# A first chunk of 128 whole tokens and 256 split ones for 384 whole ones, the sign of the weights by ScalarE, packed left-over values, queries by tile, and new due dates

## The chip, the cores and the metric

One core of one Trainium2 chip. The metric is the device time of one execution in microseconds (us). Three runs of the kernel before gave 630.63, 631.63 and 631.82 us: a median of 631.63.

TensorE (PE) multiplies, VectorE (DVE), ScalarE (ACT) and GpSimd (POOL) do the elementwise work, and SyncE (SP) issues the DMAs. Each engine takes its own instructions in the order of the program.

## What is computed

Attention over pooled keys and values, then a channel mix with a token shift. There are 8 batches of 576 tokens, 8 heads of 64; 8 keys (and values) are averaged into one, which leaves 72.

```
k_p = k.reshape(B, H, Sp, pool, D).mean(axis=3)
v_p = v.reshape(B, H, Sp, pool, D).mean(axis=3)
attn = softmax(scale * q @ k_p.T)
x = (attn @ v_p)                      # as (B, S, 512)
x_prev = x shifted by one token, zero at the start of a batch
xk = mu_k * x + (1.0 - mu_k) * x_prev
xr = mu_r * x + (1.0 - mu_r) * x_prev
k = np.maximum(xk @ w_k, 0.0)         # 512 -> 1024
v = k * k @ w_v                       # 1024 -> 512
r = 1.0 / (1.0 + np.exp(-(xr @ w_r)))
return r * v
```

The weights come as float64 words.

## The kernel before

The 4608 tokens are one row, cut into 12 chunks of 384 (`CHUNKS`, L32); a chunk is 3 tiles of 128. For each tile, `softmax` (L600) multiplies queries and keys into the bank `sc` (L620), takes maxima (L633), subtracts (L651), exponentiates (L656) and normalizes (L670, L676); `transposed` (L684) and `transposed_rest` (L714) turn the probabilities of the first 64 keys (`pm`) and of the 8 left-over keys (`px`) over. For each chunk, `attended` (L762) multiplies them with the values (L794), `shifted` (L801) scales by 1 - mu (ScalarE, L807), shifts, and joins with mu times x (VectorE, L826). `hidden` (L848) is the product with w_k (L870), with relu (L880) and square (L884 or L887); `gate` (L901) that with w_r (L919) and the sigmoid; `mixed` (L931) that with w_v (L951), then the product with the gate (L960) and the store (L964).

A matmul is done in one of two ways. **Split**: each operand is kept as a high part, rounded to the type fp32r, and the rest as a low part, and three matmuls (high x high, low x high, high x low) are summed. **Whole**: one fp32 matmul, which the trace shows as two records. Split operands need work elsewhere: `x_parts` (L838) rounds on ScalarE (L842) and subtracts on GpSimd (L844); the hidden values are rounded (L893) and subtracted (L895); each of the 20 weight tiles goes through `split` (L478; L491 and L494). Chunk 0 is whole (`WHOLE`, L35), so that it can start before the weights are split; the others are split.

Each weight tile lands as float64 words and goes through `convert` (L447) first: ScalarE takes the absolute value of the upper word, scaled (L460); VectorE shifts it (L462), joins the sign of the upper word to it (L464), and joins the bits of the lower word (L469). Whole matmuls read the result (`got_wk`, `got_wr`, `got_wv`).

The means over 8 are sums: by TensorE with a unit matrix (`summed`, L503 to L512), or by three halvings on VectorE or GpSimd (L501), as `SUM_BY` says. The left-over values (`vr`) come as three copies in 96 partitions. Loads go through SP in the order of `LOADS` (L39), keys and values into one of three `stage` buffers or into `early` ones, which use tiles of later chunks.

The order on each engine is no code order. `Order` (L112 to L213) runs all steps as threads: among the steps that could start next on an engine, that with the lowest due date goes first, and a fixed program for each engine comes out. A step's due date is worked out from its chunk, plus its entry in `EARLIER`. Of all TensorE steps those of later chunks' softmax and attended values are dated `SPARE` after their inputs.

## Time and profile before

| | us |
|---|---|
| median of the runs shown | 631.63 (630.63 to 631.82) |
| span of the profiled execution, first to last instruction | 629.5 |
| PE busy / weight loads | 615.7 / 533.1 |
| DVE / ACT / POOL busy | 402.1 / 354.6 / 208.2 |
| chain that ended last, by line | L951 32%, L870 29%, L919 14%, L794 5%, L620 5% |

The profiled execution's own time is not listed apart; against the three runs, 1.1 to 2.3 us lie around its span. Matmuls are pipelined and their ends are modelled, so a busy TensorE row says that matmuls follow each other and not how fast; the distance between starts says that. A row "x64 | 21.9, 491 | 2.3" is a count, busy us, mean ns of one, and the idle us ahead of them with what ended it.

### The profile page before, as it was taken

How to read it: one execution, taken by the hardware profiler on the slowest of the kernel's cores; microseconds unless marked ns; L12 is line 12 of the kernel's file. 1: busy time of each engine (PE TensorE's matmuls, PEld its weight loads, DVE VectorE, ACT ScalarE, POOL GpSimd, SP SyncE). 2: the span in 40 equal slices, each digit the busy share in tenths (PEclk: the TensorE clock that was granted, in tenths of full speed). 3: DMA queues.
4: the chain of work that ended last, by engine and by line, in shares of the span. 5: the costliest groups of instructions: out<-in, count | busy, mean ns of one | idle time of the engine just before them, and what ended most of it. 6: DMA issues, size and time to landing. Idle time of an engine off the chain costs nothing.

```text
span 629.5 us, 8993 instructions
## 1 busy us (share of the span) xinstructions
PE 615.7 (98%) x3210; PEld 533.1 (85%) x3210; DVE 402.1 (64%) x786; ACT 354.6 (56%) x778; POOL 208.2 (33%) x324
## 2 busy tenths in 40 slices
...
GB/s 315 340 403 171 34 35 51 35 76 142 94 51 158 59 51 51 2 143 108 18 18 51 42 187 55 3 18 56 133 98 33 35 18 33 18 2 33 18 2 50
DMA packets 34989, 50.92 MB, mean 81 GB/s; under 512 B 6528, under 2 KB 22912, under 8 KB 34944
## 3 DMA queue, kind: packets, MB, share of 16 engines
...
q14 instruction: 20, 0.16, 0.1%
...
## 4 chain that ended last, share of the span: by engine, by line
PE 88%; DMA 6%; DVE 5%; SPq 1%; issue 0%; DVEq 0%
PE mm L951 32%; PE mm L870 29%; PE mm L919 14%; PE bank L794 5%; PE sc L620 5%; DMA got_wk<-in_w_k 4%; PE bank L695 2%; DMA got_wv<-in_w_v 1%; DVE tmp L464 1%; DVE got_wr L469 1%; PE bank L750 1%; SPq L421 0%; DVE got_wv L469 0%; DVE tmp L462 0%; DVE ptl L708 0%
## 5 line engine op out<-in xcount | busy, mean ns | idle before, releaser
L870 PE MATMUL mm<-xkh,w_k 128*128 128x384 f32 x704 | 182.3, 339 | 0.0
L951 PE MATMUL mm<-w_v,sh 128*128 128x512 f32 x528 | 171.7, 393 | 0.0
L870 PEld LDWEIGHTS mm<-xkh,w_k 128*128 128x128 f32 x704 | 125.6, 188 | 1.5 <-issue 0.6
L870 PE MATMUL mm<-xkl,w_k 128*128 128x384 f32 x352 | 118.0, 335 | 0.0
L951 PEld LDWEIGHTS mm<-w_v,sh 128*128 128x128 f32 x528 | 99.3, 188 | 19.5
L951 PE MATMUL mm<-w_v,sl 128*128 128x512 f32 x264 | 103.1, 390 | 0.0
L919 PE MATMUL mm<-w_r,xrh 128*128 128x512 f32 x264 | 86.3, 397 | 0.0
L807 ACT ACTIVATE t<-bank,om_sb 128x384 f32<-128x384 f32 x96 | 49.1, 580 | 46.7 <-PE bank L794 46.6
L893 ACT CAST sh<-rk 128x384 fp32r<-128x384 f32 x88 | 45.2, 513 | 51.9 <-DVE rk L887 51.4
L670 POOL TENSOR_TENSOR px<-e,sm 128x64 f32<-128x64 f32 x31 | 9.6, 310 | 189.8 <-DVE sm L664 189.8
L960 DVE TENSOR_TENSOR rs<-mm,rs 128x512 f32<-128x512 f32 x36 | 24.7, 687 | 74.7 <-PE mm L951 74.6
L826 DVE SCALAR_TENSOR_TENSOR xm<-bank,mu_sb,t 128x384 f32<-128x384 f32 x88 | 51.1, 612 | 31.8 <-POOL t L819 15.4
L895 DVE TENSOR_TENSOR sl<-rk,sh 128x384 fp32r<-128x384 f32 x88 | 53.3, 610 | 21.3 <-ACT sh L893 21.2
L870 PEld LDWEIGHTS mm<-xkl,w_k 128*128 128x128 f32 x352 | 66.1, 188 | 0.0
L887 DVE SCALAR_TENSOR_TENSOR rk<-mm,rk 128x384 f32<-128x384 f32 x88 | 48.5, 552 | 22.7 <-ACT rk L880 21.9
L501 POOL TENSOR_TENSOR stage<-stage 128x512 f32<-128x512 f32 (+5 forms) x60 | 52.9, 887 | 25.5 <-DMA stage<-in_vm 14.8
L844 POOL TENSOR_TENSOR xkl<-xm,xkh 128x384 fp32r<-128x384 f32 x44 | 45.5, 1034 | 48.0 <-ACT xkh L842 47.6
L919 PEld LDWEIGHTS mm<-w_r,xrh 128*128 128x128 f32 x264 | 49.7, 188 | 10.1
L951 PEld LDWEIGHTS mm<-w_v,sl 128*128 128x128 f32 x264 | 49.7, 188 | 8.9
L880 ACT ACTIVATE rk<-mm 128x384 f32<-128x384 f32 x88 | 42.9, 487 | 22.1 <-PE mm L870 21.1
L919 PE MATMUL mm<-w_r,xrl 128*128 128x512 f32 x132 | 51.5, 390 | 0.0
L620 PE MATMUL sc<-kbd,qs 128*128 128x144 f32 (+1 forms) x312 | 40.6, 289 | 5.4 <-ACT e L642 3.2
...
## 6 DMA issues: line engine op xcount, KB each, us to landing
out<-rs SPq DMA_DIRECT2D x36, 256.0 KB, 2.0
stage<-in_kT SPq DMA_DIRECT2D x15, 576.0 KB, 4.9
qs<-in_qT SPq DMA_DIRECT2D x32, 256.0 KB, 3.3
stage<-in_vm SPq DMA_DIRECT2D x14, 512.0 KB, 5.4
got_wk<-in_w_k SPq DMA_DIRECT2D x8, 512.0 KB, 10.0
got_wv<-in_w_v SPq DMA_DIRECT2D x8, 512.0 KB, 10.1
...
got_wr<-in_w_r SPq DMA_DIRECT2D x4, 512.0 KB, 9.7
```

Source lines behind the costliest of these rows:

```text
L501: nc_eng.tensor_tensor(out=st[:, :, :w], in0=st[:, :, :w], in1=st[:, :, w:2 * w], op=ALU.add)
L620: nc.tensor.matmul(out=halves[g // 2][o:o + n, 0, k:k + 2 * KEYS], lhsT=qs[:, g, o:o + n], rhs=kbd[b % 2][:, g, :], start=True, stop=True,)
L807: nc.scalar.activation(out=t[:, m, 1:n + 1], in_=xp, func=AF.Copy, scale=om_sb[:, m, g:g + 1])
L826: nc.vector.scalar_tensor_tensor(out=xm[:, :n], in0=xp, scalar=mu_sb[:, m, g:g + 1], in1=t[:, m, :n], op0=ALU.mult, op1=ALU.add,)
L844: nc.gpsimd.tensor_tensor(out=lo, in0=xm[:, :n], in1=hi, op=ALU.subtract)
L870: nc.tensor.matmul(out=hp, lhsT=w[:, o], rhs=x[:, ct, :n], start=(ct == 0 and k == 0), stop=(ct == NCT - 1 and k == len(terms) - 1),)
L880: nc.scalar.activation(out=rk[:, :n], in_=hp, func=AF.Relu)
L887: nc.vector.scalar_tensor_tensor(out=rk[:, :n], in0=hp, scalar=0.0, in1=rk[:, :n], op0=ALU.max, op1=ALU.mult)
L893: nc.scalar.copy(out=sh[:, :n], in_=rk[:, :n])
L895: nc.vector.tensor_tensor(out=operand("sl", c)[:, jt, :n], in0=rk[:, :n], in1=sh[:, :n], op=ALU.subtract)
L919: nc.tensor.matmul(out=bank, lhsT=x[:, ct, o], rhs=w, start=(ct == 0 and k == 0), stop=(ct == NCT - 1 and k == len(terms) - 1),)
L951: nc.tensor.matmul(out=bank, lhsT=s[:, o], rhs=w, start=(jt == 0 and k == 0), stop=(jt == NJT - 1 and k == len(terms) - 1),)
```

## The change

Chunk 0 is cut in two: 128 tokens, whole, and 256, split. `WHOLE_ATT` keeps attended values whole for both; the other products of the 256 are split. The whole chunk's operands now lie in two of the three stage buffers, which hold no load until its gate and its mix are done. The sign of a weight comes from ScalarE: Prelu with a slope of -2^32 for Abs, which shows up in the bits that the shift leaves, and VectorE's instruction at L464 goes. The left-over values of the first two batches come packed in 128 partitions (128 KB each) and are summed by two matmuls. Queries come by tile in one DMA. Tile 0's softmax is done in two halves. Keys summed on VectorE or GpSimd go straight to their place (L674). The joins of the whole chunk are dated apart (`later_joined`). Constants come in one DMA, some costs of the planner differ, and all due dates are new.

```diff
-CHUNKS = [384] * 12
+CHUNKS = [128, 256] + [384] * 11
...
 WHOLE = (0,)
+WHOLE_ATT = (0, 1)
+TWICE = 3
+PACKED = (0, 1)
+SPREAD_ON_ACT = (0,)
+HALVED = (0,)
+EARLY = (("sl", 2), ("xrl", 1))
...
+    "k0 k1 r1 c0 r0 q0 wk0 q1 v0 q2 v1 wk1 wk2 wk3 wk4 q4 k2 q3 wk5 k3 wk6 wk7 wr0 wr1 wr2 wr3 q5 "
+    "wv2 wv0 wv1 wv3 wv4 wv5 wv6 v3 v2 wv7 "
...
-SUM_BY = {
-    "k0": "t", "k1": "v", "v0": "t", "v1": "t", "r0": "t", "k2": "v", "k3": "v", "v2": "g", "v3": "v",
-    "r1": "g",
+SUM_BY = {"k0": "t", "k1": "v", "v0": "t", "v1": "t", "r0": "t", "k2": "g", "k3": "v", "v2": "g", "v3": "v", "r1": "g"}
...
-BY_HEAD = (0, 2)
-SQUARED_ON_ACT = 8
+BY_HEAD = ((0, 1),)
+SQUARED_ON_ACT = (8, 0)
...
-    "transposed_rest 6": 4.1, "hidden 2 5": -6.4, "convert r 1": -3.5, "mixed 0 1": -9.9,
+    "warm": 898.1, "constants": 928.6, "complements": 703.7, "loads": 690.8, "keys 0 0": 871.9,
...
-SPARE = 2.4
-SECOND = 13.3
-FIRST = 22.0
+PLAN = ""
+SPARE = 0.5
+SECOND = 0.0
+NEXT = 14.0
+ATT = [0.0, 10.0]
+FIRST = 15.0
...
+    packed = {0: const.tile([P, 2, 2, D], F32, name="packed")}
-    vbd_w = sb.tile([P, NPAIR, P], F32, name="vbd_w", tag="xkl")
+    vbd_w = sb.tile([P, NPAIR, P], F32, name="vbd_w", tag="ptl")
...
-    slots("stage", 3, [P, 2 * POOL * KEYS])
+    stage = [const.tile([P, 2 * POOL * KEYS], F32, name=f"stage{i}") for i in range(3)]
+    order.give("stage", stage[0])
+    first = CHUNKS[0]
+    whole_x = stage[1][:, :2 * NPAIR * (first + 1)].rearrange("p (m g n) -> p m g n", m=2, g=NPAIR)
+    whole_operands = {
+        "xkh": whole_x[:, 0], "xrh": whole_x[:, 1],
+        "sh": stage[2][:, :NJT * first].rearrange("p (j n) -> p j n", j=NJT),
+        "pth": const.tile([P, NPAIR, first], F32, name="whole_pth"),
+        "ptr": const.tile([REM, 2, first], F32R, name="whole_ptr"),
...
+            nc.sync.dma_start(out=given, in_=consts)
...
-            yield "sp", 0.6 * len(tiles[i][2]), False
-            for b, s, n, o in tiles[i][2]:
-                nc.sync.dma_start(out=qs[:, :, o:o + n], in_=qT[b, :, :, s:s + n])
+            yield "sp", 0.6, False
+            nc.sync.dma_start(out=qs, in_=qT[i])
...
+        if kind == "r" and i in PACKED:
+            st = None
+            if i not in packed:
+                st = yield take("stage")
+                packed[i] = st[:, :4 * D].rearrange("p (k g n) -> p k g n", k=2, g=2)
+            yield "sp", 0.6, False
+            nc.sync.dma_start(out=packed[i], in_=vp[PACKED.index(i)])
+            held["r", i] = st
+            order.fetched(("r", i), 128)
...
-        nc.scalar.activation(out=ff, in_=top.bitcast(F32), func=AF.Abs, scale=REBASE)
+        nc.scalar.activation(out=ff, in_=top.bitcast(F32), func=AF.Prelu, scale=REBASE, alpha=-2.0 ** 32)
         yield "dve", 0.335, True
         nc.vector.tensor_scalar(out=t, in0=t, scalar1=3, scalar2=None, op0=ALU.logical_shift_left)
-        yield dve(WP)
-        nc.vector.scalar_tensor_tensor(
-            out=t, in0=top, scalar=-0x80000000, in1=t, op0=ALU.bitwise_and, op1=ALU.bitwise_or
-        )
...
+        eng = SUM_BY.get(f"k{2 * b + p}", "v")
+        if eng != "t":
+            raw, v = held.pop(("k", 2 * b + p))
+            on = nc.vector if eng == "v" else nc.gpsimd
+            for n in (4, 2):
+                yield (dve if eng == "v" else pool)(2 * n * KEYS)
+                halve(on, v, KEYS, n)
+            yield ("dve", 0.284, True) if eng == "v" else ("pool", 0.87, True)
+            for h2 in range(2):
+                r = slice(h2 * D, (h2 + 1) * D)
+                on.tensor_tensor(
+                    out=kbd[b % 2][r, gs, h2 * KEYS:(h2 + 1) * KEYS],
+                    in0=v[r, :, :KEYS], in1=v[r, :, KEYS:2 * KEYS], op=ALU.add,
+                )
+            done_with("stage", raw)
+            order.make(("keys", b, p))
+            return
...
+    def value_parts(b, p):
+        i, gs = b % 2, slice(2 * p, 2 * p + 2)
+        yield need(("values", b, p), ("values clear", 1))
+        yield act(2 * P)
+        nc.scalar.copy(out=vbd_h[i][:, gs], in_=vbd_w[:, gs])
+        yield dve(2 * P)
+        nc.vector.tensor_tensor(
+            out=vbd_l[i][:, gs], in0=vbd_w[:, gs], in1=vbd_h[i][:, gs], op=ALU.subtract
+        )
+        order.make(("value parts", b, p))
...
+        if b in PACKED:
+            kind, raw = "mm", (yield take("mm"))
+            yield pe(2 * D, True, 2)
+            o = raw[:REM, :2 * D].rearrange("p (g n) -> p g n", g=2)
+            for k in range(2):
+                nc.tensor.matmul(out=o, lhsT=pick, rhs=packed[b][:, k], start=(k == 0), stop=(k == 1))
...
+        if b in SPREAD_ON_ACT:
+            yield "act", 0.84, False
+            for o in range(4):
+                nc.scalar.activation(
+                    out=vbd_r[i][:, :, o], in_=vq, func=AF.Copy, scale=mask_sb[:, o:o + 1]
+                )
...
+            yield from part(i, 0, 1)
+        else:
+            yield from part(i, 0, 2)
...
+    def part(i, a0, a1):
+        parts, na = tiles[i][2], a1 - a0
+        mine = slice(a0, a1)
+        yield need(("scoring", i))
+        sc, pair, halves = held["halves", i]
+        yield need(*[("keys", b, p) for b, *_ in parts for p in range(a0, a1)])
...
-        twice = c <= 1
+        on_act = i in COPIES_ON_ACT
+
+        twice = i < TWICE
...
+        bank = yield take("mm" if c in WHOLE and g == NPAIR - 1 else "bank")
+        t = None if c in WHOLE else (yield take("t"))
...
+        ts = [operand(f"x{'kr'[m]}h", c)[:, g] if whole else t[:, m] for m in range(2)]
...
+    def later_joined(c, g):
+        yield need(("x", c, g, 0))
+        yield from joined(c, g, 1)
...
+    def joined(c, g, m):
+        n = CHUNKS[c]
+        whole = c in WHOLE
+        bank, t = held["t", c, g]
+        if whole:
+            xm = operand(f"x{'kr'[m]}h", c)[:, g]
+            ts = xm[:, :n]
+        else:
+            xm = yield take("xm")
+            ts = t[:, m, :n]
+        yield "dve", 0.134 + n / 960, False
+        nc.vector.scalar_tensor_tensor(
+            out=xm[:, :n], in0=bank[:, :n], scalar=mu_sb[:, m, g:g + 1], in1=ts, op0=ALU.mult, op1=ALU.add,
+        )
...
-        yield need(("full" if whole else "parts", "k", jt))
+        yield need(("full" if whole else "parts", "k", jt), *([("x", c, 0, 0)] if c < 2 else []))
...
+        if last and whole:
+            order.give("stage", stage[1])
...
+        if last and whole:
+            order.give("stage", stage[2])
...
+    vp = vr[list(PACKED)].reshape(-1, 4 * KR, 2, 4, 2, D).transpose(0, 3, 1, 4, 2, 5).reshape(-1, P, 2, 2, D)
+    qT = qT.transpose(2, 0, 1, 3)
```

What this makes of the order on TensorE, around the first hidden matmuls. `got_wk` are whole w_k tiles, `xkh` and `stage_107` the operand of chunk 0, `bank<-pth,vbd_w` attended values. Before:

```order
L695 MATMUL bank_114<-ident,pm_90 128x128 x4
L620 MATMUL sc_112<-kbd_69,qs_104 128x144 x4
L695 MATMUL bank_113<-ident,pm_91 128x128 x4
L740 MATMUL bank_115<-ident,pr_94 96x128 x2
L794 MATMUL bank_114<-pth_308,vbd_w 128x384
L794 MATMUL bank_114<-ptr_270,vbd_r_76 128x384
L794 MATMUL bank_113<-pth_308,vbd_w 128x384
L794 MATMUL bank_113<-ptr_270,vbd_r_76 128x384
L870 MATMUL mm_117<-xkh_361,got_wk_165 128x384
```

And now:

```order
L643 MATMUL mm_119<-early_xrl,ident 128x128 x8
L802 MATMUL sc_113<-kbd_68,qs_105 128x144 x4
L643 MATMUL mm_119<-stage_106,ident 128x128 x4
L950 MATMUL bank_116<-ident,pr_94 96x128 x2
L905 MATMUL bank_115<-ident,pm_90 128x128 x4
L643 MATMUL mm_119<-stage_106,ident 128x128 x4
L1003 MATMUL bank_114<-whole_pth,vbd_w 128x128
L1003 MATMUL bank_114<-whole_ptr,vbd_r_76 128x128
L1003 MATMUL bank_116<-whole_pth,vbd_w 128x128
L1003 MATMUL bank_116<-whole_ptr,vbd_r_76 128x128
```

Attended values stand behind one tile's transposes (`pm_90`) and the second value sum (`stage_106`), where three tiles' transposes stood; four pairs of them, then the first hidden matmul, follow.

On VectorE, in the middle of the weights' conversions. Before, a piece that follows the last join of chunk 0:

```order
L826 SCALAR_TENSOR_TENSOR xkh_361<-bank_114,mu_sb,t_82 128x384
L826 SCALAR_TENSOR_TENSOR xrh_363<-bank_114,mu_sb,t_82 128x384
L469 SCALAR_TENSOR_TENSOR got_wk_197<-got_wk_197,tmp_102 128x512
L469 SCALAR_TENSOR_TENSOR got_wk_178<-got_wk_178,tmp_101 128x512
```

And now, also from the last join of chunk 0 on:

```order
L1056 SCALAR_TENSOR_TENSOR stage_107<-mm_117,given,stage_107 128x128
L843 TENSOR_TENSOR e_89<-sc_113,mx_97 128x576
L597 TENSOR_SCALAR tmp_102<-tmp_102 128x512
L632 TENSOR_TENSOR stage_106<-stage_106 128x2x288
L625 TENSOR_TENSOR w_k_395<-got_wk_168,w_k_395 128x512
L632 TENSOR_TENSOR stage_106<-stage_106 128x2x144
L600 SCALAR_TENSOR_TENSOR got_wk_185<-got_wk_185,tmp_102 128x512
L674 TENSOR_TENSOR kbd_69<-stage_106 64x2x72 x2
L597 TENSOR_SCALAR tmp_101<-tmp_101 128x512
L1056 SCALAR_TENSOR_TENSOR xm_83<-bank_116,given,t_82 128x256
```

A conversion is two rows now (L597, L600), and splits (L625) and the joins of the 256-token chunk (`xm`, 128x256) stand between conversions. GpSimd's share of the splits, and the left-overs of the 256-token chunk, stand early too:

```order
L674 TENSOR_TENSOR kbd_69<-stage_106 64x2x72 x2
L625 TENSOR_TENSOR w_k_351<-got_wk_143,w_k_351 128x512
L1027 COPY t_82<-carry 128x2
L1029 COPY carry<-t_82 128x2
L1027 COPY t_81<-carry 128x2
L1029 COPY carry<-t_81 128x2
L1074 TENSOR_TENSOR xkl_431<-xm_83,xkh_430 128x256
L625 TENSOR_TENSOR w_k_448<-got_wk_174,w_k_448 128x512
L1074 TENSOR_TENSOR xrl_455<-xm_84,xrh_454 128x256
```

This is a piece of GpSimd's order now; in before's order its first split is the 26th row, behind the sums of r1 and v2 and chunk 0's carries.

More of the change, by code (lines that the diff above doesn't have):

```diff
@@ L286, in operand, with every, before, free_of_early @@
     def operand(kind, c):
+        if c in WHOLE:
+            return whole_operands[kind]
         if (kind, c) not in operands:
-            dtype = F32 if c in WHOLE and kind != "ptr" else F32R
+            dtype = F32 if kind == "pth" and c in WHOLE_ATT else F32R
             operands[kind, c] = sb.tile(shapes[kind], dtype, name=f"{kind}_{c}", tag=kind)
         return operands[kind, c]
+    starts = [sum(CHUNKS[:c]) for c in range(len(CHUNKS))]
+    def every(kind, c):
+        n = {"attended": NPAIR, "hid": NJT}.get(kind, CHUNKS[c] // P)
+        return [(kind, c, k) for k in range(n)]
+    def before(kind, c):
+        return every(kind, c - 1) if c > 1 else []
+    def free_of_early(c, tag):
+        return [("early", t, i) for t, n in EARLY for i in range(n) if t == tag and c not in WHOLE]
     slots("rs", CH // P, [P, DM])
@@ L323, in attention_then_channel_mix @@
     slots("mm", 3, [P, 512], pool=banks)
-    starts = [sum(CHUNKS[:c]) for c in range(len(CHUNKS))]
     def stretches(at, n):
@@ L542, in values @@
         i = b % 2
[L543 to L544 removed]
+        whole = b == 0 and 0 in WHOLE_ATT
+        yield need(("v", 2 * b + p), *(every("attended", last_chunk[b - 2]) if b > 1 else [("values clear", b)]))
         if not b:
@@ L686, in transposed @@
         o = slice(off, off + P)
-        yield need(("pm", i), *([("attended", c - 1)] if c else []))
-        if c == 1:
-            yield need(("early", "ptl", 0))
+        yield need(("pm", i), *before("attended", c))
+        if c == len(WHOLE_ATT):
+            yield need(*[("value parts", 0, p) for p in range(2)])
         pm = held.pop(("pm", i))
@@ L796, in attended, with shifted @@
                 )
-        if g == NPAIR - 1:
-            order.make(("attended", c))
-        yield from shifted(c, g, (0, 1), bank, t, True)
-    def shifted(c, g, ms, bank, t, last):
+        order.make(("attended", c, g))
+        yield from shifted(c, g, bank, t)
+    def shifted(c, g, bank, t):
         n = CHUNKS[c]
```

347 lines of the change are left out of this document (193 added, 154 removed), and 172 rows, old and new, of the table EARLIER.

## The prediction

> **What bounds the kernel now.** I read the page first: busy shares and the chain that ended last. Then the busy time by stretches, to see whether that bound holds everywhere.
>
> ```profile
> span 629.5 us, 8993 instructions
> ...
> PE 615.7 (98%) x3210; PEld 533.1 (85%) x3210; DVE 402.1 (64%) x786; ACT 354.6 (56%) x778; POOL 208.2 (33%) x324
> ...
> PE 88%; DMA 6%; DVE 5%; SPq 1%; issue 0%; DVEq 0%
> ```
>
> ```profile
> 0.00:15.00 15.00, 9.01 (x49) 7.83 (x50) 7.92 (x20) 6.16 (x23) 2.15 (x9) 0.99 0.90 317
> 15.00:80.00 65.00, 61.03 (x254) 37.76 (x253) 62.64 (x143) 45.57 (x105) 13.66 (x23) 0.98 0.66 232
> 80.00:100.00 20.00, 20.00 (x86) 13.37 (x85) 13.98 (x25) 11.00 (x23) 15.68 (x22) 1.00 0.16 55
> 100.00:600.00 500.00, 499.94 (x2712) 453.00 (x2711) 313.51 (x595) 288.55 (x623) 176.74 (x271) 1.00 0.18 58
> ```
>
> Columns: PE, weight load, DVE, ACT, POOL, clock, DMA share, GB/s. From 100 us on TensorE has no gap (499.94 of 500), so there only a smaller amount of matmul work can gain. Before 80 it has gaps, and from 15 to 80 VectorE is the full engine (62.64 of 65). So there are two questions: how much TensorE work goes, and what VectorE's queue then allows in the first 80 us.
>
> **TensorE work, part by part.** Ends of matmuls are pipelined, so a step is (length of a piece, less the mean length of one) / (count - 1).
>
> ```profile
> 42.71 7.58 PE L870 MATMUL mm<-xkh,got_wk 128*128 128x384 f32 x23
> 73.48 9.84 PE L951 MATMUL mm<-got_wv,sh 128*128 128x512 f32 x22
> 23.07 1.15 PE L620 MATMUL sc<-kbd,qs 128*128 128x144 f32 x8
> 20.23 1.04 PE L512 MATMUL mm<-early_ptl,ident 96*96 96x128 f32 x8
> ```
>
> ```profile
> L870 PE MATMUL mm<-xkh,got_wk 128*128 128x384 f32 x64 | 21.9, 491 | 2.3 <-DVE xkh L826 2.3
> L951 PE MATMUL mm<-got_wv,sh 128*128 128x512 f32 x48 | 21.8, 598 | 0.2 <-DVE got_wv L469 0.2
> ```
>
> ```profile
> 235.99 1.77 PE bank L794 x16
> 584.56 16.66 PE mm L870 x96
> 601.23 8.20 PE mm L919 x36
> 609.43 16.33 PE mm L951 x72
> ```
>
> Whole (fp32) matmuls are two records each: 0.322 us a record at 384 columns, 0.43 at 512 ((9.84 - 0.60) / 21 = 0.44, and 0.43 where no other piece follows at once), 0.12 at 144, 0.11 at 128. Split matmuls: 16.66 / 96 = 0.174 at 384, 8.20 / 36 and 16.33 / 72 = 0.227 at 512, 1.77 / 16 = 0.11 at 192.
>
> Removed with the whole chunk of 384: hidden 64 x 0.322 = 20.6, gate 24 x 0.43 = 10.3, mix 48 x 0.43 = 20.6, its attended values 8 x 0.323 + 4 x 0.174 = 3.3, left-over sums 16 x 0.11 = 1.8, six three-copy transposes 0.7. Together 57.3.
>
> Added, 128 whole and 256 split: hidden 64 x 0.11 = 7.0 and 96 x 0.121 = 11.6; gate 8 x 0.43 + 24 x 0.227 = 8.9; mix 16 x 0.43 + 48 x 0.227 = 17.8; attended values 3.5; left-over sums 8 x 0.11 = 0.9; three two-copy transposes 0.3. Together 50.0. The trace has no split matmul of 256 columns. It lies between the rows of 192 (0.11) and 384 (0.174); I take 0.121, on the line through 384 and 512, which lies near the row of 192. The ends make -1.1 to +5.1 us. The whole hidden matmul of 128 columns lies between 0.11 and 0.322; I take the row of the same width. The net is 50.0 - 57.3 = **-7.3 us**. The other chunks keep their matmuls.
>
> **The first 80 us.** Before, the split hidden of the next chunk starts at 94.58. The matmuls that stand ahead of it, each at its step, sum to 79.9, so 14.7 us were lost: waits, and a slow clock.
>
> ```profile
> 94.58 4.17 PE mm L870 x24
> ```
>
> ```profile
> PE sc L620 <- ACT e L642: 3.2, 1, 3.2
> PE mm L870 <- DVE xkh L826: 2.3, 2, 1.8
> PE sc L620 <- DMA qs<-in_qT: 1.4, 1, 1.4
> ```
>
> For after I follow VectorE, since it is full. Its first join for chunk 0 (before: at 28.62) needs one tile's softmax instead of three.
>
> ```profile
> 10.00:15.00 5.00, 1.81 (x14) 1.60 (x13) 4.48 (x14) 3.71 (x18) 0.00 (x0) 0.98 1.03 408
> 25.55 0.91 PE L794 MATMUL bank<-pth,vbd_w 128*128 128x384 f32 x2
> 28.02 0.68 DVE L464 SCALAR_TENSOR_TENSOR tmp<-got_wk,tmp 128x512 int32<-128x512 int32 x1
> 28.62 0.61 DVE L826 SCALAR_TENSOR_TENSOR xkh<-bank,mu_sb,t 128x384 f32<-128x384 f32 x1
> 29.14 0.68 DVE L469 SCALAR_TENSOR_TENSOR got_wk<-got_wk,tmp 128x512 int32<-128x512 int32 x1
> 83.13 1.52 DVE L469 SCALAR_TENSOR_TENSOR got_wv<-got_wv,tmp 128x512 int32<-128x512 int32 x1
> L462 DVE TENSOR_SCALAR tmp<-tmp 128x512 int32<-128x512 int32 x20 | 8.0, 417 | 1.3 <-ACT tmp L460 1.3
> ```
>
> ```profile
> stage<-in_kT SPq DMA_DIRECT2D x15, 576.0 KB, 4.9
> qs<-in_qT SPq DMA_DIRECT2D x32, 256.0 KB, 3.3
> stage<-in_vm SPq DMA_DIRECT2D x14, 512.0 KB, 5.4
> got_wk<-in_w_k SPq DMA_DIRECT2D x8, 512.0 KB, 10.0
> ```
>
> The last input to land is now the second half of the values. Up to and with it stand two key loads, three queries, one weight tile, two value loads and 0.3 MB of packed left-overs and constants, 3.8 MB: at 0.4 MB/us (408 GB/s) from about 3.5 us on, it lands at 13. Its sums and copies, in the new order behind a transpose, take until 16.7, and from attended values to first join before took 28.62 - 25.55 = 3.1. So the join comes at about 19.7. If TensorE lost as much ahead of its attended values as before (25.55 - 16.6 of steps = 9.0 against my 3.3), it would be 25.4; I take the walk, since one tile needs no second and third round of exponentials (the 3.2 above), and keep 25.4 as an end.
>
> From this join to the split of the last w_v tile, the order holds 55.4 us of VectorE steps: 16 shifts at 0.335, 16 second halves at 0.60 (28.02 to 28.62), 11 splits at 0.60, 16 softmax passes at 0.67, joins 5.8, the square and left-over of the 256-token chunk 5.3, others. The sign by ScalarE removes 20 instructions of 0.60, 12.0 us, 16 of them from this stretch. ScalarE's Abs of the same size is replaced by one Prelu; a Prelu is not in the trace, and I take the same price, between nothing more and 1.28 more each if it called for a table. The order has two table loads more in all and none beside a Prelu, and ScalarE is 45.57 of 65 busy.
>
> Before, the same kind of stretch, 28.62 to the end of the last conversion at 84.6, held 50.8 us of steps in 56.0, a factor of 1.10. So after, the last split ends at 19.7 + 55.4 x 1.10 = 80.6. TensorE reaches the matmul that reads it with 66.7 us of steps done: 13.9 lost by then, against 14.7: **-0.8 us**. So the freed VectorE time does not shorten the stretch: splits that lay behind 84 us move into it. Factor 1.0 gives 75.1, so -6.3.
>
> Two waits are added in SP's queue, since two of the three stage buffers now hold chunk 0's operands. The load k3 waits for GpSimd's sum of k2, and behind it stand the last two w_k tiles and all of w_r and w_v; v2 waits for chunk 0's gate, and behind it stands the last w_v tile. By the same walk k2 lands at 20 and its sum (1.25 + 0.75 + 0.9 on GpSimd) ends at 23, so the next w_k tile lands at 28.5, and VectorE's queue comes to it at 32: 3 us of cover. The gate ends at 52, the last w_v tile lands at about 57.5, VectorE comes to it at 63: 5 us of cover. I book nothing; if a cover is gone, VectorE is late by what lacks, at most some 3 us.
>
> **After 100 us.** The new dates put the hidden rows closer:
>
> ```profile
> 601.32 0.49 ACT L880 ACTIVATE rk<-mm 128x384 f32<-128x384 f32 x1 [0.45 <-PE mm L870]
> 601.85 0.56 DVE L887 SCALAR_TENSOR_TENSOR rk<-mm,rk 128x384 f32<-128x384 f32 x1 [0.38 <-ACT rk L880]
> 625.86 0.69 DVE rs L960
> ```
>
> A bank is free 1.35 us after its last matmul (601.06 to 602.41). In before's order 72 of 80 hidden groups from the third chunk on leave 4.1 us or more of other matmuls until their bank is used again; in after's 25 of 88 do, 37 leave 2 to 3 us, and 7 leave 1.36 to 1.8. The spare stays positive, but one VectorE instruction of 0.7 ahead in the queue uses half of it. I book +1.0, between -1.5 (half of what before lost after 95 us: 629.5 - 607.6 of steps - 14.7 - 4.1 at the end = 3.1) and +6 (0.07 for each of the 88). The wider queries (one DMA a tile) and the packed left-over values lie beside TensorE after 100 us: the DMA share there is 0.18. The end (last product to last store, 625.86) is in the same order.
>
> Sum against the profiled span: 629.5 - 7.3 - 0.8 + 1.0 = 622.4. The shown runs have a median of 631.63, 2.1 above that span, so **624.5 us**.
>
> **Rivals.** *VectorE runs without delays* (factor near 1.0). For it: its early waits fall from three tiles to one. Price: -6.3 instead of -0.8, up to 619.0.
>
> *A new wait on the port that VectorE and GpSimd share*: the other side.
>
> ```profile
> L895 DVE TENSOR_TENSOR sl<-rk,sh x88: 506/558/2297, 100.6 to 603.0; 128x384 fp32r<-128x384 f32 x88
> L494 POOL TENSOR_TENSOR w_k<-got_wk,w_k 128x512 fp32r<-128x512 f32 x3 | 4.3, 1419 | 8.3 <-ACT w_k L491 8.3
> ```
>
> The same subtraction takes 506 ns, or up to 2297 where a GpSimd instruction stands beside it; the last w_v conversion above took 1.52 instead of 0.68. Between first join and last split the order of after has 24 us of GpSimd steps (splits at about 1.25, the chunk's left-overs, a key sum), before's 10. If all 14 more block VectorE, its last split ends at 95, and the time is 639. It is slower than before once 7 of the 14 do. The Trainium skill, "SBUF — State Buffer", section "Who interferes with whom", says that a VectorE instruction with two SBUF inputs and a GpSimd instruction that reads SBUF exclude each other for the whole instruction. The rows agree in kind; taken at its word, every such pair that meets is paid for in full, and the sum would be nearer to 639. Against it: VectorE has 24 of its 55 us in instructions that read PSUM or reduce, beside which GpSimd can run.
>
> *The clock falls in the new early gaps.*
>
> ```profile
> 15.00:16.00 1.00, 1.00 (x7) 1.00 (x6) 1.00 (x5) 0.71 (x2) 0.00 (x0) 0.50 1.08 243
> 14.84 3.55 PE L512 MATMUL mm<-stage,ident 128*128 128x128 f32 x16
> 18.44 1.95 PE L512 MATMUL mm<-early_sl,ident 128*128 128x128 f32 x16
> ```
>
> After the wait of 3.2 us the granted clock was 0.50, and 16 sums took 3.55 instead of 1.95: 1.6 us. By after's order the gaps up to 20 us are shorter but many. Two such falls cost 3.2: 627.7. The Trainium skill, "TensorE: Matmul & The Clock Gate", Part 1, has the gate fall after an idle window of about 3.4 us; by that rule gaps of 1 to 2 us bring none, and before's own loss of 1.6 would go.
>
> *The close hidden rows lose time* in every chunk: +6 instead of +1, 629.5.
>
> *The change does not bring its work saving*: narrow matmuls are held by their weight loads, 0.174 at 256 columns and 0.16 at 128: +8, 632.5.
>
> **How the numbers follow.** Forecast 0.48; VectorE without delays 0.20; shared port 0.10; clock 0.06; close rows 0.11; narrow matmuls 0.05. About 0.2% is what a measurement of this kernel tells from no change: 630.4 to 632.9. Faster: 0.46 of the forecast, 0.20, 0.06, half of the close rows and 0.03 of the port: 0.81. Slower: 0.06 of the port, 0.02 of the narrow matmuls: 0.08. Same: 0.11. The range goes from the fast rival's 619 to 631.5, a little past the close rows; it leaves out most of the shared port and the narrow matmuls.
>
> **What would show it.** The first hidden matmul at about 20 us, not 29; split hidden records of 256 columns at 0.12 a step; the last w_v split at about 80 us with VectorE busy from 20 on; from 100 us on TensorE busy in full. Wrong: VectorE subtractions of over 1 us in the first 80 us in large number, a clock of 0.50 after 20 us, or waits of hidden rows on L1116 in each chunk.

## The result: slower by 1.4%

The changed kernel takes **640.58 us** (median of 4 runs, 639.61 to 641.22) where the kernel before took 631.13 beside it (4 runs, 629.83 to 631.82): a ratio of 1.0138, with a 95% interval of 1.0106 to 1.0169. The forecast was 624.5, the range 619 to 631.5. The profiled execution took 639.61 us, 1.8 more than its span.

The page of the changed kernel: the span, the busy shares, the chain that ended last by engine.

```profile
span 637.8 us, 9268 instructions
...
PE 614.8 (96%) x3331; PEld 544.9 (85%) x3331; DVE 405.8 (64%) x800; ACT 357.4 (56%) x773; POOL 218.9 (34%) x346
...
PE 71%; DVE 14%; POOL 5%; issue 5%; ACT 4%; DMA 1%; SPq 0%; POOLq 0%; DVEq 0%; ACTq 0%
```

TensorE is busy for no longer than before (615.7), but its share fell from 98 to 96%, and the chain runs over it for 71% instead of 88. Where the gaps are is shown by the busy times of the same stretches as before (TensorE, weight load, VectorE, ScalarE, GpSimd, then clock, DMA share, GB/s):

```profile
0.00:15.00 15.00, 12.06 (x76) 10.88 (x77) 9.78 (x28) 6.63 (x22) 3.80 (x14) 1.00 0.89 317
15.00:80.00 65.00, 57.34 (x337) 46.53 (x337) 63.73 (x145) 53.01 (x131) 30.18 (x41) 0.95 0.58 212
80.00:100.00 20.00, 18.36 (x112) 16.20 (x111) 17.89 (x36) 13.63 (x29) 14.48 (x28) 1.00 0.23 83
100.00:600.00 500.00, 492.97 (x2651) 442.07 (x2651) 305.56 (x580) 276.72 (x579) 170.43 (x264) 1.00 0.18 59
```

Two things changed. From 15 to 80 us VectorE is as full as before (63.7 of 65), and ScalarE (45.6 to 53.0) and GpSimd (13.7 to 30.2) have more to do; TensorE has fewer busy microseconds (57.3 against 61.0). And from 100 to 600 us TensorE, which had no gap before (499.94 of 500), now has 7.0 us of them. What ended them (TensorE's rows of the view of waits; total, number, longest):

```profile
PE mm L1100 <- DVE stage L1056: 2.7, 2, 1.6
PE bank L960 <- DVE pr L942: 2.6, 2, 1.4
PE mm L1100 <- DVE rk L1116: 2.0, 3, 1.4
PE mm L1100 <- ACT stage L1109: 1.8, 2, 1.0
...
PE bank L960 <- DVE xm L1056: 1.2, 1, 1.2
PE bank L960 <- DVE ptl L918: 0.9, 1, 0.9
PE mm L1181 <- ACT rs L1156: 0.9, 1, 0.9
...
PE mm L1100 <- ACT xkh L1072: 0.4, 1, 0.4
```

The rows of before name no wait of L750, its transpose of the left-over weights. Now the same transpose (L960) waits five times, for 5.3 us with a row of 0.6 for ScalarE (4.0 of them behind 100 us), and hidden rows (L1100) three times for the release of their bank.

**A balance.** Each TensorE record taken at its step as in the prediction (0.12 for 256 columns split), the work is the sum of the steps, and what the clock shows beyond it is lost:

| profile | work | lost by 30 us | 30 to 60 | 60 to 100 | behind 100 |
|---|---|---|---|---|---|
| before | 607.8 | 9.7 | 2.1 | 1.3 | 2.9 |
| changed | 600.6 | 9.3 | 6.2 | 3.4 | 12.7 |

7.2 us of work are gone. 5.8 more are lost by 100 us and 9.8 more behind it (head and tail add 0.05): 15.6 - 7.2 = 8.4 against 8.3 between the spans. At 100 us the changed kernel has 520.8 us of TensorE work ahead of it, and the kernel before 522.3: nearly all that was saved has by then been given back.

### The profile page after: what moved, and what is told of

Its sections match the earlier page's. It is cut to its first block, busy times and chain, and to the rows that moved or that the text cites. A ratio compares the mean times of both kernels' runs of the same rounds, so it can differ in the third digit from the quotient of the medians.

```text
span 637.8 us, 9268 instructions
## 1 busy us (share of the span) xinstructions
PE 614.8 (96%) x3331; PEld 544.9 (85%) x3331; DVE 405.8 (64%) x800; ACT 357.4 (56%) x773; POOL 218.9 (34%) x346
## 4 chain that ended last, share of the span: by engine, by line
PE 71%; DVE 14%; POOL 5%; issue 5%; ACT 4%; DMA 1%; SPq 0%; POOLq 0%; DVEq 0%; ACTq 0%
PE mm L1100 25%; PE mm L1181 21%; PE mm L1148 14%; PE sc L802 4%; PE bank L1003 3%; POOL xkl L1074 2%; DVE xm L1056 2%; PE bank L905 2%; POOL xrl L1074 1%; DVE sm L851 1%; DVE e L843 1%; DVE rk L1116 1%; DMA got_wv<-in_w_v 1%; DVE vbd_l L705 1%; DVE stage L632 1%
## 5 line engine op out<-in xcount | busy, mean ns | idle before, releaser
L1100 PE MATMUL mm<-xkh,w_k 128*128 128x384 f32 (+1 forms) x768 | 195.1, 336 | 3.4 <-DVE rk L1116 2.0
L1100 PEld LDWEIGHTS mm<-xkh,w_k 128*128 128x128 f32 x768 | 135.6, 188 | 6.7 <-DVE rk L1116 2.9
L1100 PE MATMUL mm<-xkl,w_k 128*128 128x384 f32 (+1 forms) x384 | 127.1, 331 | 0.6 <-POOL xkl L1074 0.6
L1056 DVE SCALAR_TENSOR_TENSOR xm<-bank,given,t 128x384 f32<-128x384 f32 (+1 forms) x96 | 54.2, 599 | 76.3 <-POOL t L1031 45.7
L1074 POOL TENSOR_TENSOR xkl<-xm,xkh 128x384 fp32r<-128x384 f32 (+1 forms) x48 | 47.8, 998 | 126.7 <-ACT xkh L1072 121.5
L1016 ACT ACTIVATE t<-bank,om_sb 128x384 f32<-128x384 f32 (+1 forms) x96 | 48.9, 570 | 43.9 <-PE bank L1003 43.5
L1100 PEld LDWEIGHTS mm<-xkl,w_k 128*128 128x128 f32 x384 | 72.2, 188 | 1.1 <-POOL xkl L1074 1.1
L1122 ACT CAST sh<-rk 128x384 fp32r<-128x384 f32 (+1 forms) x96 | 48.2, 504 | 44.4 <-DVE rk L1116 44.1
L1124 DVE TENSOR_TENSOR sl<-rk,sh 128x384 fp32r<-128x384 f32 (+1 forms) x96 | 52.7, 552 | 23.4 <-ACT sh L1122 22.8
L1116 DVE SCALAR_TENSOR_TENSOR rk<-mm,rk 128x384 f32<-128x384 f32 (+1 forms) x96 | 51.6, 541 | 25.1 <-ACT rk L1109 24.4
L1109 ACT ACTIVATE rk<-mm 128x384 f32<-128x384 f32 (+1 forms) x96 | 45.9, 481 | 36.2 <-PE mm L1100 32.0
L632 POOL TENSOR_TENSOR stage<-stage 128x512 f32<-128x512 f32 (+7 forms) x59 | 51.1, 869 | 3.2 <-DVE pr L942 0.5
L1074 POOL TENSOR_TENSOR xrl<-xm,xrh 128x384 fp32r<-128x384 f32 (+1 forms) x48 | 48.3, 1007 | 3.3 <-ACT xrh L1072 3.1
```

The lines of the kernel that those rows point to most:

```text
L632: nc_eng.tensor_tensor(out=st[:, :, :w], in0=st[:, :, :w], in1=st[:, :, w:2 * w], op=ALU.add)
L1016: nc.scalar.activation(out=ts[m][:, 1:n + 1], in_=xp, func=AF.Copy, scale=om_sb[:, m, g:g + 1])
L1056: nc.vector.scalar_tensor_tensor(out=xm[:, :n], in0=bank[:, :n], scalar=mu_sb[:, m, g:g + 1], in1=ts, op0=ALU.mult, op1=ALU.add,)
L1074: nc.gpsimd.tensor_tensor(out=lo, in0=xm[:, :n], in1=hi, op=ALU.subtract)
L1100: nc.tensor.matmul(out=hp, lhsT=w[:, o], rhs=x[:, ct, :n], start=(ct == 0 and k == 0), stop=(ct == NCT - 1 and k == len(terms) - 1),)
L1109: nc.scalar.activation(out=rk[:, :n], in_=hp, func=AF.Relu)
```

## The experiments

All ratios are to the kernel before, with 95% intervals.

**Cover ahead of transposes and scores, in the kernel before.** `SPARE` is the time that the planner keeps between the result that a TensorE step waits for and that step.

```
-SPARE = 2.4
+SPARE = 0.5
```

> The kernel before, with one number changed: the spare time that its planner keeps ahead of a step of scores, transposes or attended values on TensorE, 2.4 -> 0.5 us (chunks 2 and on). The work is the same. Theory A (cover: the change lost its 9.7 us after 100 us because these steps stand too close behind the VectorE instructions that they wait for, while the contention on VectorE is about the same as before): TensorE loses 6 to 10 us more after 100 us, in waits of about 1 us at transposes of left-over or main weights; 637 to 641 us. Theory B (the contention itself, or the number of GpSimd instructions, is what grew with the change): cover matters little here, 630 to 633 us.

638.18 us, 1.0094 (1.0071 to 1.0118), with 8.5 us lost behind 100 us instead of 2.9. The time is theory A's; the loss grew by 5.6, a little less than the 6 to 10 of that theory. The place of the longest wait, by the timeline (start, length) and then in stretches:

```profile
112.93 1.03 POOL L676 TENSOR_TENSOR pm<-e,sm 128x512 f32<-128x512 f32 x1
113.20 0.82 DVE L730 CAST pr<-px 128x64 fp32r<-128x64 f32 x1
113.93 1.26 POOL L494 TENSOR_TENSOR w_v<-got_wv,w_v 128x512 fp32r<-128x512 f32 x1
114.61 0.66 DVE L732 TENSOR_TENSOR pr<-px,pr 128x64 fp32r<-128x64 f32 x1
115.33 0.33 PE L750 MATMUL bank<-ident,pr 128*128 128x128 f32 x1 [2.18 <-DVE pr L732]
```

```profile
113.00:116.00 3.00, 0.82 (x7) 0.68 (x7) 3.00 (x6) 1.20 (x4) 2.19 (x2) 1.00 0.00 0
116.00:119.00 3.00, 3.00 (x11) 3.00 (x11) 2.96 (x8) 2.92 (x7) 0.00 (x0) 0.51 0.09 14
```

Two small VectorE instructions stand beside GpSimd's and take 0.82 and 0.66 us; the transpose behind them waits 2.18 us; and then TensorE's granted clock falls to 0.51 for three microseconds, which costs 1.5 more. The same meetings were there before (its 42 casts of this line take 537 ns on the mean); then TensorE had other work in front of the transpose.

**Cover in the changed kernel.** In its table every step has a written date, and another spare alone would list the early part anew too. So two kernels were run: both keep the written dates up to chunk 3 (softmax and transposes up to tile 8) and leave the rest to the planner; one has 2.4 us of spare from chunk 4 on, the other 0.5.

```
-        spare = SPARE if tiles[i][0] > 1 else 0.0
+        spare = 2.4 if tiles[i][0] > 3 else SPARE if tiles[i][0] > 1 else 0.0
```

(and the same for the attended values)

> The changed kernel with due dates of its table kept up to chunk 3 and tile 8, the planner's own dates behind, and from chunk 4 on 2.4 us of spare ahead of scores, transposes and attended values instead of 0.5. The work is the same; by the planner's own idle times TensorE's gaps behind 100 us are 3 us longer than in the changed kernel. Theory A (cover): the loss behind 100 us falls from 12.6 to 7 or 8 us all the same; 634 to 637 us, with hardly a transpose that waits over 0.5 us from chunk 4 on. Theory B (contention): the waits stay, and the planned gaps come on top; 641 to 645 us.

> The kernel with late cover (635.5 us) with that cover taken back to 0.5 us, so that only its due dates differ from the changed kernel's: the table up to chunk 3 and tile 8, the planner's own dates behind. Theory A (cover): the loss behind 100 us is 11 us or more again, with transposes and scores that wait about 1 us; 638.5 to 642 us. Theory B (the written due dates of the late chunks, not the cover, were at fault): the loss behind 100 us stays at 8 us or less; 634 to 636.5 us.

With the cover 635.49 us, 1.0055 (1.0038 to 1.0072), and 7.9 us lost behind 100 us; with the dates alone 638.50 us, 1.0098 (1.0078 to 1.0119), and 10.4, a little under theory A's 11. TensorE's stretches of the one with cover, and of the one without:

```profile
100.00:200.00 100.00, 96.88 (x520) 85.19 (x520) 74.28 (x145) 59.28 (x127) 42.29 (x62) 1.00 0.33 104
200.00:600.00 400.00, 399.99 (x2160) 362.37 (x2159) 228.85 (x443) 216.24 (x459) 130.25 (x206) 1.00 0.14 47
```

```profile
100.00:200.00 100.00, 96.14 (x519) 83.98 (x519) 77.69 (x149) 64.74 (x136) 42.91 (x63) 1.00 0.31 102
200.00:600.00 400.00, 398.95 (x2144) 360.38 (x2143) 233.79 (x435) 213.88 (x449) 129.09 (x204) 1.00 0.14 48
```

For comparison, the changed kernel itself, which has 4.6 of its 7.0 us of gaps behind 200 us:

```profile
100.00:200.00 100.00, 97.55 (x528) 86.22 (x528) 74.67 (x149) 59.42 (x126) 42.39 (x61) 1.00 0.32 104
```

With 2.4 us of cover TensorE has no gap from 200 us on, as theory A had it. But without the cover, with the dates alone, the gaps there are already down from 4.6 to 1.1 us: behind 200 us most of the loss went with the written dates, as theory B had it. From 100 to 200 us the gaps are 2.5 us in the changed kernel, 3.9 with the dates alone (1.2 of them at one score, put down to its query load) and 3.1 with cover. What the cover itself does is seen at the transposes of left-over weights: behind 100 us they wait 4.0 us in the changed kernel, 1.9 with the dates alone and not at all with cover. In their place hidden rows and gates wait 2.2 us for a square (0.4 with the dates alone). What stays with cover lies between 100 and 200 us. The cover is worth 0.4% (the intervals 1.0038 to 1.0072 and 1.0078 to 1.0119 don't meet). The dates alone moved the ratio from 1.0138 to 1.0098, which the intervals don't separate.

**The planner's price of a split matmul**, 2 ns lower in the change, an edit that the prediction did not price: alone, and with the spare of 0.5, in the kernel before.

```
-    return "pe", times * (... max(0.111, n / 2400 + 0.0155)), False
+    return "pe", times * (... max(0.111, n / 2400 + 0.0135)), False
```

> The kernel before with the planner's price of a split matmul lowered by 2 ns, from n/2400 + 15.5 ns to n/2400 + 13.5 ns, as the change has it. The work is the same; the planner's sum of TensorE steps falls from 616.5 to 611.8 us, where the trace has 607.8. Theory A (the price is a second cover: a planned step that is longer than the real one gives VectorE time that the plan doesn't know of): the loss behind 100 us grows by 1 to 4 us, 632.5 to 636. Theory B (the price only shifts the plan): 631 to 632.5.

> The kernel before with both: the lower price and 0.5 us of spare. Theory A (price and spare are both cover, and they make up the 9.8 us that the changed kernel loses more behind 100 us): the loss behind 100 us, 8.5 with the spare alone, goes to 11 to 14 us; 640 to 644 us. Theory B (the spare alone): 637 to 639.

633.00 us, 1.0003 (0.9987 to 1.0018), and 637.79, 1.0088 (1.0068 to 1.0108), with 4.0 and 8.1 us lost behind 100 us. The first time and its loss, 1.1 us more than before, lie at the low end of theory A's, but the ratio can't be told from 1. The second is theory B's: with the spare of 0.5 the lower price adds nothing to the loss of 8.5 us. So the price explains 1 of the 9.8 us at most.

**The sign by ScalarE alone, in the kernel before.** Every other instruction keeps its place.

```
-        nc.scalar.activation(out=ff, in_=top.bitcast(F32), func=AF.Abs, scale=REBASE)
+        nc.scalar.activation(out=ff, in_=top.bitcast(F32), func=AF.Prelu, scale=REBASE, alpha=-2.0 ** 32)
...
-        nc.vector.scalar_tensor_tensor(
-            out=t, in0=top, scalar=-0x80000000, in1=t, op0=ALU.bitwise_and, op1=ALU.bitwise_or
-        )
```

> The kernel before with one part of the change alone: the sign of the weights is made by ScalarE's one pass (Prelu with slope -2^32 in place of Abs), and VectorE's 20 instructions for it are gone; every other instruction stands in the order of before. Theory A (VectorE is the bound from its first join to the last conversion): the last conversion comes 8 to 10 us earlier, and TensorE gets back 2 to 4 of the 14.6 us lost by 95 us, no more, because only 3.4 of them are lost behind 30 us; 627 to 629.5 us. Theory B (ScalarE pays for it: the Prelu calls for a table or is longer than the Abs): the conversions wait for ScalarE, 631 to 640 us.

**627.76 us, 0.9938 (0.9915 to 0.9961): faster than both kernels.** The time is theory A's, the way to it only in part. VectorE from 28 to 80 us, and its shift ahead of a conversion with what it waited for (busy, mean ns, idle before):

```profile
28.00:80.00 52.00, 49.89 (x177) 28.13 (x178) 46.02 (x95) 36.26 (x74) 12.42 (x21) 1.00 0.57 214
```

```profile
L460 ACT ACTIVATE tmp<-got_wk 128x512 f32<-128x512 f32 x8 | 5.4, 673 | 1.8 <-DMA got_wk<-in_w_k 1.7
L462 DVE TENSOR_SCALAR tmp<-tmp 128x512 int32<-128x512 int32 x20 | 11.4, 575 | 4.0 <-ACT tmp L460 3.7
...
81.22 1.53 DVE L466 SCALAR_TENSOR_TENSOR got_wv<-got_wv,tmp 128x512 int32<-128x512 int32 x1
```

VectorE is 46.0 us busy, where it was 51.1 in the same stretch before, and now its shift waits 3.7 us for ScalarE's first pass (1.3 before). The last conversion came at 81.22 instead of 83.13: 1.9 us earlier, not 8 to 10. The Prelu itself takes 673 ns where the Abs took 672.

> The kernel before with the sign by ScalarE, and 3.4 us of spare instead of 2.4. Theory A (more cover helps further): TensorE's loss behind 100 us, 2.7 us, falls by 1; 627. Theory B (2.4 covers what there is to cover): the same as with the sign alone, 627.5 to 629.

With `SPARE = 3.4` on top: 633.19 us, 1.0016 (1.0001 to 1.0031), and 8.3 us lost behind 100 us where the sign alone has 2.7. Neither theory: more spare lists the work anew too, and hidden rows then wait for their banks (1.7 us at one place). So spare is not good by itself; a list made with it has to be seen on the chip.

**The half clock at 22 us.** Eleven matmuls that add zero were put into the gap ahead of it.

```
+            early = (c, jt) == (0, 0)
+            for k in range({0: 6, 1: 5}.get(ct, 0) if early else 0):
+                nc.tensor.matmul(out=hp, lhsT=vbd_h[1][:, 0].bitcast(F32), rhs=ident, start=(ct == 0 and k == 0), stop=False)
```

> The changed kernel with 11 matmuls of a zero block added into the first hidden group, 6 ahead of its first and 5 ahead of its second input row, 22 records in which TensorE would else wait for the first joins (19.5 to 23 us). Nothing else is changed. Theory A (the half clock between 22 and 28.5 us costs what it takes from TensorE): the granted clock stays at 1.00, and the time falls by about 3 us, to 637.5. Theory B (VectorE's queue is full from 14 to 69 us, so TensorE would have waited for it anyway): the clock stays at 1.00, and the time falls by less than 1 us, 639.6 to 640.6.

642.13 us, 1.0161 (1.0133 to 1.0189): no gain. Two stretches, in the changed kernel and with the added matmuls:

```profile
22.00:28.00 6.00, 5.00 (x22) 4.98 (x23) 5.97 (x17) 3.14 (x6) 5.03 (x8) 0.50 0.31 98
...
43.00:47.00 4.00, 3.28 (x23) 2.83 (x23) 3.93 (x11) 4.00 (x12) 3.68 (x6) 1.00 1.01 404
```

```profile
22.00:28.00 6.00, 5.94 (x46) 5.24 (x45) 5.97 (x16) 4.21 (x11) 4.89 (x9) 1.00 0.36 106
...
43.00:47.00 4.00, 3.82 (x17) 3.53 (x18) 3.77 (x11) 3.04 (x10) 3.83 (x5) 0.57 1.03 410
```

From 22 to 28 us the clock stays at 1.00. But VectorE is full in both (5.97 of 6): at 28 us TensorE now waits 0.98 for a left-over conversion, where it had not waited, and by 30 us it is only 0.7 us further in its own work than in the changed kernel, not 3 (an estimate by the steps). So far this is theory B. The time lies above both theories' ranges, and the rows of 43 to 47 us show a part of the reason: the clock falls there instead, to 0.50 from 43.2 to 46.6 us, which costs about 1.7 us (half of 3.4, an estimate). From 30 to 60 us 2.1 us more are lost in all, with a wait of 1.07 at 51 us for a square (0.3 before). So the run tells what the clock from 22 to 28 us is worth, and not what a clock of 1.00 throughout would be.

**What fills the first 85 us of the changed kernel.** Four kernels take work from the engines beside TensorE, one gives work back to VectorE; the order is held in all. Without GpSimd's splits of weights:

```
+            nc.gpsimd.memset(low[kind, i].bitcast(F32), 0.0)
```

> The changed kernel; the low parts of the nine weight tiles that GpSimd splits are left out (set to zero by a GpSimd memset of about 0.52 us, in place of a subtraction of 1.28). VectorE's work and the order are unchanged. Theory A (contention: VectorE's long instructions stand beside these subtractions): of the 6.9 us by which VectorE's instructions are longer than alone between the first join and the last w_v split, 3.4 stood beside a split by GpSimd; they go, the last w_v split ends 3 us earlier, and the time falls by 2 to 3.5 us, to 637 to 638.5. Theory B (VectorE's own work alone fills the stretch): the last split moves by less than 1 us, 640 to 641 us.

> The same kernel as the one without GpSimd's weight splits, once more for its trace: where its VectorE time went, since its time was that of the changed kernel. Theory A: VectorE's long instructions went (3 us or less of them ahead of the last w_v split), and TensorE waits elsewhere, for ScalarE. Theory B: the long instructions stand beside other GpSimd work now, 6 us or more.

With the squares of chunk 1 on ScalarE, and with no instruction in their place:

```
+            if c == 1:
+                nc.scalar.activation(out=rk[:, :n], in_=rk[:, :n], func=AF.Square)
```

> The changed kernel; the squares of the 256-token chunk, eight VectorE instructions of 0.41 us, are made by ScalarE at the same places of the order. Theory A (VectorE's queue bounds TensorE up to 70 us, and ScalarE has room): VectorE has 3.3 us less ahead of the last w_v split; the time falls by 2 to 3.5 us, to 637 to 638.5. Theory B (ScalarE, 33.9 of 40 us busy between 20 and 60, becomes the bound): no gain or slower, 640 to 643 us.

> The changed kernel; the squares of the 256-token chunk are left out (its hidden rows stay at their relu), so eight VectorE instructions of 0.41 us are gone and ScalarE has nothing more to do. Theory A (VectorE's queue itself bounds the first 70 us; moving the squares to ScalarE failed only because ScalarE then was late): the last w_v second half ends 2 to 3 us earlier, and the time falls by 2 to 3 us, to 637.5 to 638.5. Theory B (VectorE, ScalarE and TensorE wait for one another in turn, and 3 us off one of them is taken up by a wait for the next): less than 1 us, 639.6 to 641.

> The squares of the 256-token chunk and GpSimd's nine weight splits both left out. Theory A: VectorE has 3.3 us less of its own and 2.6 us less in long instructions; 634.5 to 637. Theory B: 638 to 641.

With the sign by VectorE (Abs in place of Prelu):

```
+        nc.vector.scalar_tensor_tensor(
+            out=t, in0=top, scalar=-0x80000000, in1=t, op0=ALU.bitwise_and, op1=ALU.bitwise_or
+        )
```

> The changed kernel with one part of the change undone: the sign of the weights is made by VectorE again, 20 more instructions of 0.60 us in its queue, one ahead of each second half, everything else in the order of the changed kernel. Theory A (VectorE's queue bounds the stretch here, so each microsecond counts): some 17 of them stand ahead of the last w_v split, and TensorE is later by 7 to 10 us; 647 to 651 us. Theory B (as in the kernel before, where taking the same 12 us out of VectorE's queue moved its last conversion by only 1.9 us, because the weights then came late): 643 to 645 us.

| kernel | us | ratio (interval) | lost 30 to 100 us | behind 100 |
|---|---|---|---|---|
| changed | 640.58 | 1.0138 (1.0106 to 1.0169) | 9.6 | 12.7 |
| without GpSimd's splits | 640.48 | 1.0135 (1.0113 to 1.0158) | 8.8 | 13.4 |
| squares by ScalarE | 642.12 | 1.0170 (1.0143 to 1.0196) | 11.2 | 13.7 |
| squares left out | 639.41 | 1.0122 (1.0095 to 1.0149) | 8.1 | 14.0 |
| both left out | 640.45 | 1.0127 (1.0098 to 1.0155) | 9.5 | 14.7 |
| sign by VectorE | 660.86 | 1.0458 (1.0434 to 1.0482) | 23.6 | 16.1 |

(The losses of the second row are from that kernel's second run, 640.13 us.) The times of the four that take work away are theory B's or within 0.2 us of it: none of these reliefs gains anything that can be told from zero. Two things go into that. Without GpSimd's splits and with the squares left out, 0.8 and 1.5 us less are lost from 30 to 100 us, but 0.7 and 1.3 more behind 100 us, so that what is gained early is given back late. And with both left out the granted clock of the profiled execution fell twice more, to 0.50 from 58.9 and from 413.9 us on for 3.4 us each; up to 1.7 us of each of its two losses is that. No run took work from ScalarE. Without GpSimd's splits VectorE's long instructions ahead of the last w_v split fell from 6.9 to 4.3 us, between what the two theories said, and its waits rose from 1.3 to 3.1, the longest, 1.6, for ScalarE's copy of a weight tile. With the squares on ScalarE, VectorE waited 1.27 for a ScalarE copy that it had not waited for. The other way there is no such give: 20 instructions of 0.60, 12.0 us, cost 20 us, more than theory A had. TensorE's longest waits in that kernel:

```profile
PE mm L1103 <- DVE stage L1059: 6.2, 2, 3.7
PE mm L1184 <- DVE got_wv L603: 3.5, 2, 3.3
PE mm L1151 <- DVE rk L1119: 3.2, 1, 3.2
```

The longest of each is over 3 us, and the granted clock fell to 0.74 from 20 to 40 us and to 0.83 from 60 to 80, so that waits cost twice here: as idle time and as a slower clock behind them.

> Both at once: the late cover of 2.4 us (which gave 635.5) and the squares of the 256-token chunk on ScalarE. If the early loss and the late loss are apart from one another, the gain of the squares comes on top: 632 to 633.5 us by theory A of the squares alone, 635 to 637 by theory B.

Late cover and squares on ScalarE together: 635.73 us, 1.0061 (1.0042 to 1.0080), the same as the cover alone (1.0055): theory B. The cover with the squares left out was not tried.

## Why the prediction was wrong, step by step

**TensorE's work: right.** -7.3 was forecast, 607.8 - 600.6 = 7.2 measured. The split matmul of 256 columns, which the trace of before didn't have, runs at 0.12 (the rows below are six records apart, 0.71 us), and the whole one of 128 at 0.11. Weight loads held neither.

```profile
55.45 0.40 PE L1100 MATMUL mm<-xkh,w_k 128*128 128x256 f32 x2
55.69 0.28 PE L1100 MATMUL mm<-xkl,w_k 128*128 128x256 f32 x1
55.81 0.40 PE L1100 MATMUL mm<-xkh,w_k 128*128 128x256 f32 x2
56.04 0.28 PE L1100 MATMUL mm<-xkl,w_k 128*128 128x256 f32 x1
56.16 0.40 PE L1100 MATMUL mm<-xkh,w_k 128*128 128x256 f32 x2
```

**The walk along VectorE's queue: right in kind, too short.** Its marks in the timeline, the first join and the last w_v split:

```profile
20.74 0.34 DVE L1056 SCALAR_TENSOR_TENSOR stage<-bank,given,stage 128x128 f32<-128x128 f32 x1
...
84.40 0.68 DVE L625 TENSOR_TENSOR w_v<-got_wv,w_v 128x512 fp32r<-128x512 f32 x1
```

The join was forecast at 19.7, the last split to end at 80.6; it ends at 85.1. Between them VectorE has 56.05 us of its own steps (55.4 forecast), 6.9 us in which its instructions are longer than alone, and 1.3 us of waits: a factor of 1.15, where 1.10 was carried over from before (4.3 us long there). The split ends 4.5 us late: 1.0 of them is the join, 0.7 are steps, and 2.7 are long instructions and waits (8.2, where the factor allowed 5.5). So TensorE had lost 18.1 us by then, not 13.9, and 2.2 more by 100 us, where none were booked (both with the 1.5 us or so ahead of the first matmul, which the table above leaves out). The step that failed is that one engine's queue was taken to tell the time of the whole stretch, with a factor from another order.

From 30 to 60 us, where 4.1 of the 5.8 us more are lost, TensorE's rows hold 3.7 us of waits (0.8 for VectorE's softmax and 0.4 for a join before), and 3.1 of them end with a result of ScalarE (L1109 1.8, L1156 0.9, L1072 0.4), not of VectorE. Ahead of the two longest, 1.0 and 0.9, ScalarE is itself full: from 35.2 to 42.4 us its instructions follow each other without a gap, and at 55.8 a table load of 1.28 stands ahead of the sigmoid (L1156). The busy times of the engines, before and then changed, show how much more stands in the stretch:

```profile
0.00:20.00 20.00, 14.01 (x80) 12.83 (x81) 12.86 (x39) 10.05 (x43) 2.15 (x9) 0.91 0.94 314
20.00:60.00 40.00, 36.52 (x160) 22.89 (x159) 38.37 (x83) 27.81 (x60) 9.94 (x18) 1.00 0.85 304
60.00:100.00 40.00, 39.52 (x151) 23.24 (x149) 33.33 (x67) 24.88 (x46) 19.39 (x27) 1.00 0.18 63
```

```profile
0.00:20.00 20.00, 16.23 (x106) 14.39 (x106) 14.75 (x42) 11.04 (x33) 3.80 (x14) 1.00 0.92 326
20.00:60.00 40.00, 33.84 (x212) 28.54 (x212) 39.17 (x91) 33.86 (x86) 21.95 (x34) 0.91 0.68 256
60.00:100.00 40.00, 37.68 (x206) 30.68 (x205) 37.48 (x75) 28.37 (x65) 22.71 (x35) 1.00 0.24 86
```

By 100 us VectorE is busy for 6.8 us more (84.6 to 91.4), although the sign left it, ScalarE for 10.5 more (62.7 to 73.3) and GpSimd for 17 more (31.5 to 48.5). Over the whole span they have 3.7, 2.8 and 10.7 more, so half of this (17.1 of 34.3) is more busy time altogether, and half is work that is wanted sooner: the splits of weights, inputs and hidden rows stand ahead of the 256 split tokens, where before they stood ahead of the next chunk. TensorE was relieved in the stretch in which VectorE was already full, and the other two got the most added there. Which of them is last then changes from place to place, and none of the reliefs that were tried, of VectorE and GpSimd, was worth 2 us.

**Behind 100 us: the largest error, 8.8 of the 15.4 us between 622.4 and 637.8.** +1.0 was booked, up to +6, for hidden rows that come close behind the release of their banks. They do wait (2.0 us), but the transposes of left-over weights, for which the prediction counted nothing, wait more (4.0), and the scores 0.7. It looked at the distance between two uses of a hidden row's bank, not at the distance between VectorE's work and the transpose that waits for it, be it for its input (1.3 of the 4.0) or for its own bank (2.1). `SPARE` and the dates set that distance, and the diff shows both. A place with 1.24 us:

```profile
387.66 1.63 DVE L940 CAST pr<-px 128x64 fp32r<-128x64 f32 x2
388.22 1.02 POOL L1074 TENSOR_TENSOR xrl<-xm,xrh 128x384 fp32r<-128x384 f32 x1
389.20 1.29 POOL L632 TENSOR_TENSOR stage<-stage 128x512 f32<-128x512 f32 x1
389.21 1.50 DVE L942 TENSOR_TENSOR pr<-px,pr 128x64 fp32r<-128x64 f32 x2
...
390.94 1.14 DVE L1056 SCALAR_TENSOR_TENSOR xm<-bank,given,t 128x384 f32<-128x384 f32 x2 [0.23 <-POOL t L1031]
...
392.13 0.33 PE L960 MATMUL bank<-ident,pr 128*128 128x128 f32 x1 [1.24 <-DVE xm L1056]
```

Two pairs of VectorE instructions of 0.13 us each take 1.63 and 1.50 beside GpSimd's subtraction and sum; the two joins come late, and the transpose's bank is free only behind them. The contention is nearly that of before: behind 100 us VectorE's instructions are longer than alone by 39.5 us in sum, 35.0 before. What is new is that TensorE stands right behind. That a small spare can do this is shown in the kernel before for two transposes and the clock behind one of them (2.2, 0.8 and 1.5 of the 5.5 us), all of them between 100 and 200 us; behind 200 us a spare of 0.5 leaves no gap there (400.00 of 400). In the changed kernel the dates of the late chunks took 3.5 of the 4.6 us of gaps behind 200 us away, and the cover the rest. So the spare is one part of the late loss, and the written dates are another, the larger one behind 200 us; which dates, and why, is open. More than 5 us of lost time stay between 100 and 200 us even with late cover; there hidden rows and gates wait for squares (2.2 us) and one score 0.5, and no transpose, so cover for chunks 2 and 3 may not help. It was not tried.

**The rivals.** *The clock* fell, at 21.9 us, as that rival had it (3.1 us lost to it): after a wait of 1.55 us and 0.7 of work, as the next wait, of 1.16, began. Keeping it up until 28 us was worth 0.7 us by 30 us, with VectorE full, and it fell at 43 us instead. *The shared port* gave a time near the measured one (639) by another way: its extra cost in the first 85 us is 6.9 - 4.3 = 2.6, not 14. The Trainium skill, "SBUF — State Buffer", section "Who interferes with whom", has every such pair that meets pay in full; the long instructions above agree in kind, but by their 2.6 us only a small part of the 14 us of GpSimd steps met one. *Close hidden rows* was a third of the waits behind 100 us, 2.0 us where it had 6. *Narrow matmuls* and *VectorE without delays* did not come.

**SP's two new waits** and the covers of 3 and 5 us held: the only waits for a weight load in ScalarE's rows are 2.3 us for w_k (2.1 before) and 0.3 for w_v.

**Not settled:** how much of the early loss belongs to the chunk of 128 itself and how much to the order of its helpers; how much of the time from 30 to 60 us ScalarE alone costs, since no run took work from it. The packed left-over values and the queries by tile were not tried alone.
